# A spectral filter with a mixture of experts on one core: eight groups of batches become four

## The chip, the cores and the metric

One core of a Trainium2 chip runs the whole kernel. The metric is the device time of one execution in microseconds. Of three runs of the kernel before, the median is 1513.49 us (1512.85 to 1513.52).

## What is computed

Eight batches of 2496 positions with 256 channels are filtered along the positions: a real Fourier transform, a product with a complex filter per frequency and channel, and the transform back. Each of the 19,968 filtered rows is a token that goes to one of eight experts: the one with the largest cosine to its embedding. The expert is a 256 to 1024 to 256 network with a ReLU, and its output is scaled by the expert's softmax weight.

```python
X = np.fft.rfft(x, axis=1)                       # x: (8, 2496, 256)
y = np.fft.irfft(X * (filt_r + 1j * filt_i), n=2496, axis=1)
...
x = y.reshape(19968, 256)
logits = normalized(x) @ normalized(expert_emb).T / tau
expert_idx = np.argmax(logits, axis=1)
gate_w = softmax(logits)[np.arange(N), expert_idx]
for e in range(8):
    mask = expert_idx == e
    out[mask] = gate_w[mask, None] * (np.maximum(x[mask] @ w1[e], 0) @ w2[e])
```

## The kernel before

**The filter.** 2496 is 64 x 39, so the transform is done as two small DFTs each way. Stage one (`conv_s1`, L384) reads tiles of three times 39 positions, multiplies each with a block of DFT-39 factors, and stores the spectrum's parts to the DRAM buffer `SD`. The middle stage (`conv_s2`, L405) reads them back by frequency (`a`), does a DFT-64 product on TensorE, multiplies with the filter on VectorE (`yy` with the real, `xs` with the imaginary part, L432 and L434; `f` is the filter slice read by `load_f`, 256 KB), does the inverse DFT-64 product (`sa`), and stores to the DRAM buffer `ZD`. The last stage (`conv_sb`, L493) reads `ZD`, does the inverse DFT-39 product (`y`), normalizes and splits the rows into f16 high and low halves, transposes them (half by DMA, half on TensorE), and computes the logits. `route` (L613) turns every four tiles of logits into ranks, and GpSimd scatters each tile's rows with an indirect DMA (L697) into `XS`, a DRAM buffer with a region per expert.

A tile is always 512 columns wide. In a group of one batch it holds two blocks of rows or two frequencies of that batch; in a group of two batches (`GROUPS[g][0] == 2`) it holds one block or one frequency of both. So a step of the middle stage reads two filter slices in the first case (`k * 2 // nb`, L419), and one in the second. A product is either one f32 product, or, from a group number on (`G_S1`, `G_S2`, `G_SA`, `G_SB` for the four stages), split in three products of fp32r halves that ScalarE and VectorE make (`split`, L343).

**The experts.** `Slot` (L786) is a block of 128 or 256 tokens of one expert: rows are read transposed from `XS` (`xT`), then in four quarters of the hidden units `prep` copies weights (`wp`, VectorE), `up` multiplies (`ph`, L830), ScalarE and VectorE make the two halves of `h` (L836, L837), and `down` multiplies again (`po`, L850). ScalarE scales, GpSimd scatters the output rows (L858).

**What sets the order.** `GROUPS` says for every group how many batches it has and the size of the blocks that its tokens fill. A group that is filtered and routed adds to a queue as many full blocks as are sure to exist whatever the routing (`full_blocks`, L53, used at L86 to L94); what is left of the tokens goes to a last phase of 128-token blocks. While a queue runs, `spread` (L932) weaves steps of the next group's filter between the quarters of the blocks; `pace` divides the group's steps over the queue. The first group's filter runs alone (`head`, L890): its steps, numbered from 0, also carry the 16 weight loads (`WLOADS` gives step and number) and the 48 steps of weight preparation (`weight_halves`, L228: largest value of each matrix, scales, f16 high and low halves), at a rate given by the lines at L914. The first stage of group g + 1 is woven into the last stage of group g (`later`, L875).

With `GROUPS = ((1, 128),) + ((1, 256),) * 7` the queues are 12 blocks of 128 and 6, 10, 10, 9, 10, 10 and 10 of 256 tokens; then the last phase, in which 19 blocks of 128 run.

## Time and profile before

| | |
|---|---|
| median of 3 runs | 1513.49 us (1512.85 to 1513.52) |
| the profiled execution: its time | 1514.53 us |
| its span, first to last instruction | 1512.4 us |
| TensorE busy | 1282.9 us, 85% |
| VectorE, ScalarE, GpSimd busy | 66%, 52%, 36% |
| mean granted clock of TensorE | 0.903 of 2.4 GHz |
| bytes moved by DMA | 240.91 MB |

PE is TensorE, PEld its weight loads, DVE is VectorE, ACT ScalarE, POOL GpSimd, SP the engine that issues most DMAs. The granted clock is the share of 2.4 GHz that TensorE had on average; it has two levels, 1.2 and 2.4 GHz. A busy share over the whole span mixes three different stretches, so most of the rows below are of windows of time.

### The profile page before, as it was taken

The numbers are of one execution on the slowest core, as the hardware profiler recorded it, in microseconds if no ns is written. First come the engines' busy times: TensorE is split into PE (matmuls) and PEld (weight loads), VectorE is DVE, ScalarE is ACT, GpSimd is POOL, SyncE is SP. The second block draws the span as 40 slices with busy tenths as digits, with TensorE's granted clock in tenths as the row PEclk, the third lists the DMA queues.
The fourth block names the chain that finished last, engine by engine and source line by source line (L and its number), as shares of the span: only waits on it lengthen the run. The fifth ranks groups of instructions, "written<-read, shape, count | busy, mean of one in ns | idle before, by whom it ended". The sixth has DMA issues, their size and how long they took to land.

```text
span 1512.4 us, 36347 instructions
## 1 busy us (share of the span) xinstructions
PE 1282.9 (85%) x10678; PEld 983.3 (65%) x10678; DVE 992.1 (66%) x3238; ACT 781.9 (52%) x1781; POOL 551.1 (36%) x613
## 2 busy tenths in 40 slices
PE   4543649877998898898989997999899988999998
PEld 1111326654665576676877775787778766888998
DVE  3765658656574776696767784878578755444565
ACT  2653626643572576376735693568456732233333
POOL 0121544154425433552444435443454145121222
PEclk7765759987998898999999998999999998999999
DMA  9882858856894797577655895669465633222121
GB/s 302 304 279 64 193 145 246 187 136 190 221 192 134 212 218 148 149 215 185 161 137 154 214 206 141 166 200 207 114 182 177 132 88 89 52 52 46 43 48 41
DMA packets 278909, 240.91 MB, mean 159 GB/s; under 512 B 173977, under 2 KB 220385, under 8 KB 276933
## 3 DMA queue, kind: packets, MB, share of 16 engines
q1 hardware_dynamic: 248156, 161.38, 44.3%
q0 software_dynamic: 26400, 60.07, 13.6%
q10 hardware_dynamic: 4169, 17.12, 3.1%
q8 instruction: 102, 1.67, 0.5%
q14 instruction: 82, 0.67, 0.2%
HBM read 121.61 MB, written 84.84 MB: 137 GB/s over the span
## 4 chain that ended last, share of the span: by engine, by line
PE 55%; issue 13%; DMA 11%; DVE 10%; another core or an unknown queue 4%; ACT 4%; POOL 2%; SPq 0%; DVEq 0%; POOLq 0%; ACTq 0%
PE ph L830 20%; PE po L850 20%; PE s L382 4%; DMA out_dram<-o,meta 3%; PE y L382 2%; PE y L377 2%; PE s L377 2%; DMA f<-ZD 2%; DMA yT<-rows 2%; PE sa L382 2%; DVE wmx L235 1%; DMA f<-in_filt 1%; PE tp L584 1%; DMA SD<-s 1%
## 5 line engine op out<-in xcount | busy, mean ns | idle before, releaser
L830 PE MATMUL ph<-xT,wp 128*128 128x256 f16 (+1 forms) x4608 | 526.2, 262 | 28.7 <-issue 15.4
L850 PE MATMUL po<-W,h 128*128 x3864 | 518.4, 279 | 35.0 <-issue 25.1
L830 PEld LDWEIGHTS <-wp 128*128 128x128 f16 x4608 | 397.4, 100 | 125.6 <-issue 64.1
L850 PEld LDWEIGHTS <-h 128*128 128x128 f16 x3864 | 371.1, 100 | 118.9 <-issue 65.5
L836 ACT ACTIVATE h<-ph 128x512 f16<-128x512 f32 (+1 forms) x384 | 204.4, 533 | 311.6 <-PE ph L830 165.3
L818 DVE COPY wp<-W 128x1024 f16 x384 | 187.5, 489 | 222.0 <-PE ph L830 129.4
L858 POOL DMA_INDIRECT out_dram<-o,meta x161 | 171.5, 1065 | 390.0 <-ACT o L857 331.8
L837 DVE SCALAR_TENSOR_TENSOR h<-ph,h 128x512 f16<-128x512 f32 (+1 forms) x384 | 230.3, 600 | 50.7 <-ACT h L836 47.8
L697 POOL DMA_INDIRECT XS<-rows,ixi x176 | 177.9, 1011 | 173.9 <-issue 99.9
L468 POOL TENSOR_TENSOR yy<-yy,xs 128x512 f32<-128x512 f32 x70 | 94.5, 1351 | 113.1 <-DVE xs L434 85.7
L337 POOL DMA_DIRECT2D in<-in_x x84 | 66.3, 790 | 146.9 <-DVE xp L351 61.4
L857 ACT ACTIVATE o<-po,meta 128x256 f32<-128x256 f32 x161 | 69.8, 479 | 51.5 <-PE po L850 26.8
L536 DVE SCALAR_TENSOR_TENSOR rows<-y,rr,rows 128x256 f16<-128x256 f32 x176 | 76.9, 477 | 16.2 <-ACT rows L533 11.2
L533 ACT ACTIVATE rows<-y,rr 128x256 f16<-128x256 f32 x176 | 75.3, 492 | 21.1 <-DVE rr L570 19.2
L460 ACT COPY xs<-s 64x512 f32<-64x512 f32 x80 | 46.6, 582 | 76.4 <-PE s L377 63.7
L432 DVE TENSOR_TENSOR yy<-s,f 128x256 f32<-128x256 f32 x160 | 60.8, 416 | 37.5 <-ACT xs L461 30.2
L377 PE MATMUL s<-a,c_sb 128*128 128x512 f32 x80 | 51.5, 737 | 37.8 <-DVE yy L432 13.0
L565 ACT ACTIVATE rows<-y 128x256 f16<-128x256 f32 x176 | 67.5, 402 | 26.8 <-PE y L377 21.0
L377 PE MATMUL y<-f,csb_sb 120*128 120x512 f32 (+2 forms) x72 | 45.2, 718 | 37.3 <-issue 22.4
L434 DVE SCALAR_TENSOR_TENSOR xs<-xs,sgn_sb,f 128x256 f32<-128x256 f32 x160 | 76.1, 511 | 0.0
L400 ACT COPY s<-s 128x512 f32<-128x512 f32 x88 | 52.6, 599 | 30.1 <-DMA SD<-s 10.7
L382 PE MATMUL s<-xp,c1h 117*128 117x512 f32 (+1 forms) x144 | 62.2, 439 | 5.5 <-issue 3.3
(190 smaller groups left out, 1600.8 us busy)
## 6 DMA issues: line engine op xcount, KB each, us to landing
f<-in_filt SPq DMA_DIRECT2D x160, 256.0 KB
a<-SD SPq DMA_DIRECT2D x80, 256.0 KB
ZD<-z SPq DMA_DIRECT2D x80, 256.0 KB
SD<-s SPq DMA_DIRECT2D x80, 240.0 KB
f<-ZD SPq DMA_DIRECT2D x80, 240.0 KB
in<-in_x POOLq DMA_DIRECT2D x70, 234.0 KB
W<-in_w ACTq DMA_DIRECT2D x14, 1024.0 KB
XS<-rows,ixi POOLq DMA_INDIRECT x176
```

Of the source, the lines that this page charges most:

```text
L377: nc.tensor.matmul(out_, c[:a.shape[0]], a, start=True, stop=True)
L382: nc.tensor.matmul(out_, w[:k], b, start=(n == 0), stop=(n == 2))
L434: nc.vector.scalar_tensor_tensor(out=o, in0=i, scalar=sgn_sb[:, k2:k2 + 1], in1=f, op0=ALU.mult, op1=ALU.mult)
L468: nc.gpsimd.tensor_tensor(out=yy, in0=yy, in1=xs, op=ALU.add)
L536: nc.vector.scalar_tensor_tensor(out=rows[:, i, D:2 * D], in0=y[:, i], scalar=rr[:, u:u + 1], in1=rows[:, i, 0:D], op0=ALU.mult, op1=ALU.s ...
L697: i = nc.gpsimd.indirect_dma_start(out=XS, out_offset=bass.IndirectOffsetOnAxis(ap=ix, axis=0), in_=src, in_offset=None)
L818: last["dve"] = nc.vector.tensor_copy(wp, src[:, :, fp * 256:fp * 256 + 256])
L830: last["pe"] = nc.tensor.matmul(ph[:, fi, :size], wp[:, k * 2 + wh, fi * P:(fi + 1) * P], xT[:, xh * 2 + k], start=(c == 0), stop=(c == 5))
L836: nc.scalar.activation(h[:, 0, :, :size], ph[:, :, :size], AF.Relu)
L837: nc.vector.scalar_tensor_tensor(out=h[:, 1, :, :size], in0=ph[:, :, :size], scalar=0.0, in1=h[:, 0, :, :size], op0=ALU.max, op1=ALU.subtract)
L850: nc.tensor.matmul(self.po[:, s], self.hs[fp][:, hh, fi, s * P:(s + 1) * P], self.Wp[:, off + wh * 1024:off + wh * 1024 + D], start=(fp == ...
L858: i = nc.gpsimd.indirect_dma_start(out=out, out_offset=bass.IndirectOffsetOnAxis(ap=self.meta[:, s, 0:1].bitcast(I32), axis=0), in_=o, in_ ...
```

## The change

The groups become four of two batches each; the first has blocks of 128 tokens. The stages switch to split products at other group numbers: the first stage from group 1 (batch 2 on, as before), the other three from group 2 (batch 4 on; before, the middle stage's first product from batch 4 and the other two from batch 3). The weight loads are divided over the first 48 steps of the head instead of 33, and the weight preparation runs at one piece a step from step 16. `SMAX` limits a queue to 30 blocks, so that the table of a queue fits its buffer: the first group would have 32.

```diff
-GROUPS = ((1, 128),) + ((1, 256),) * 7
+GROUPS = ((2, 128),) + ((2, 256),) * 3
...
-G_S1, G_SB, G_S2, G_SA = 2, 3, 4, 3
+G_S1, G_SB, G_S2, G_SA = 1, 2, 2, 2
 DLAG = 2
 MID = 8
-WLOADS = {3: 1, 6: 1, 10: 2, 32: 2} | {n: 1 for n in range(12, 32, 2)}
+WLOADS = {3: 1, 6: 1, 10: 2} | {n: 1 for n in range(13, 48, 3)}
 WLATE = 6
+SMAX = 30
...
         left += n * S
-        k = full_blocks(left, size)
+        k = min(full_blocks(left, size), SMAX)
         phases.append((g, size, k, False))
...
-            if n >= 14 and not 44 <= n < 60:
-                owed += 1.5 if n < 60 else 1
+            if n >= 16:
+                owed += 1
             while owed >= 1:
                 owed -= 1
                 next(prep, None)
```

The queues are then 30 blocks of 128 and 17, 19 and 20 of 256 tokens, and the last phase as before. Line numbers after the new line are higher by one.

Two places of the order that the prediction speaks of. The first is VectorE's list in the middle stage of the head, at the filter products of step 7 (`yy_7`, `xs_7`; `W<-W` makes a low half of weights, `wmx` a largest value, `wall` waits for GpSimd). Before:

```order
L432 TENSOR_TENSOR yy_7_554<-s_0_7_549,f_14_493 128x256
L434 SCALAR_TENSOR_TENSOR xs_7_551<-xs_7_551,sgn_sb,f_14_493 128x256
L246 RECIPROCAL winv<-wsc 128x2
L235 TENSOR_REDUCE wmx<-W 128x1 x2
L241 TENSOR_SCALAR wall<-wall 128x2
L432 TENSOR_TENSOR yy_7_554<-s_0_7_549,f_15_495 128x256
L434 SCALAR_TENSOR_TENSOR xs_7_551<-xs_7_551,sgn_sb,f_15_495 128x256
```

And now:

```order
L433 TENSOR_TENSOR yy_7_606<-s_0_7_601,f_7_553 128x512
L435 SCALAR_TENSOR_TENSOR xs_7_603<-xs_7_603,sgn_sb,f_7_553 128x512
L264 SCALAR_TENSOR_TENSOR W<-W,wsc 128x1024
L242 TENSOR_SCALAR wall<-wall 128x2
L236 TENSOR_REDUCE wmx<-W 128x1 x2
L264 SCALAR_TENSOR_TENSOR W<-W,wsc 128x1024
L243 TENSOR_SCALAR wsc<-wall 128x2
L433 TENSOR_TENSOR yy_8_628<-s_0_8_623,f_8_579 128x512
```

A step had four products of 256 columns with two filter slices; it has two of 512 with one slice, and the weight work between them is the same in kind, with one piece a step.

The second is GpSimd's list while a queue of blocks runs and the last stage of the next group is routed (`XS<-rows` scatters a tile's rows, x2 for its two halves; `out_dram<-o` a block's output; `yy` is the sum of the two filter products in the middle stage). Before, in the third queue:

```order
L697 DMA XS<-rows_0_4489,ixi_0_5085 161920x258 x2
L697 DMA XS<-rows_1_4537,ixi_0_5085 161920x258 x2
L697 DMA XS<-rows_2_4638,ixi_0_5085 161920x258 x2
L697 DMA XS<-rows_3_4680,ixi_0_5085 161920x258 x2
L858 DMA out_dram<-o_3_0_5837,meta_3_4955 19968x256
L858 DMA out_dram<-o_3_1_5842,meta_3_4955 19968x256
L697 DMA XS<-rows_4_4741,ixi_4_5411 161920x258 x2
L697 DMA XS<-rows_5_4816,ixi_4_5411 161920x258 x2
L697 DMA XS<-rows_6_4879,ixi_4_5411 161920x258 x2
L697 DMA XS<-rows_7_4996,ixi_4_5411 161920x258 x2
```

And now, in the first queue:

```order
L698 DMA XS<-rows_15_6358,ixi_12_7082 161920x258 x2
L859 DMA out_dram<-o_24_0_7574,meta_24_7155 19968x256
L469 TENSOR_TENSOR yy_0_8382<-yy_0_8382,xs_0_8379 128x512
L698 DMA XS<-rows_16_6544,ixi_16_7680 161920x258
L469 TENSOR_TENSOR yy_1_8426<-yy_1_8426,xs_1_8423 128x512
L698 DMA XS<-rows_16_6544,ixi_16_7680 161920x258
L469 TENSOR_TENSOR yy_2_8455<-yy_2_8455,xs_2_8452 128x512
L698 DMA XS<-rows_17_6690,ixi_16_7680 161920x258 x2
L859 DMA out_dram<-o_25_0_7802,meta_25_7365 19968x256
L698 DMA XS<-rows_18_6817,ixi_16_7680 161920x258
```

Eight row scatters in one run were the rule, three runs to a batch; now they stand in ones and twos between output scatters and the next group's sums. Over the queues with filter work, runs of six or more hold 113 of 154 row scatters before and 21 of 132 in the change.

## Rows read from the trace of the kernel before

**Rows 1.** The profile's page: busy time of each engine with its share of the span and its instructions; and TensorE's busy share in 40 equal slices of the span, in tenths.

```profile
PE 1282.9 (85%) x10678; PEld 983.3 (65%) x10678; DVE 992.1 (66%) x3238; ACT 781.9 (52%) x1781; POOL 551.1 (36%) x613
...
PE   4543649877998898898989997999899988999998
```

**Rows 2.** Windows, cut where the first hidden product of each queue's first block is made on VectorE: the head, the seven queues that run beside a filter, the last queue, the last phase. Columns: window and its length in us, then busy us and number of instructions of each engine, granted clock, busy share of the DMA engines, GB/s.

```profile
0.00:226.80 226.80, 109.20 (x322) 42.70 (x323) 135.05 (x441) 98.43 (x180) 59.15 (x75) 0.67 0.69 215
226.80:366.40 139.60, 119.07 (x1100) 85.86 (x1098) 93.01 (x360) 73.52 (x192) 57.32 (x66) 0.88 0.74 187
366.40:494.30 127.90, 112.32 (x825) 78.20 (x822) 73.98 (x290) 66.82 (x165) 53.99 (x63) 0.92 0.76 183
494.30:675.70 181.40, 163.47 (x1267) 125.04 (x1267) 135.86 (x431) 111.57 (x253) 78.14 (x83) 0.92 0.76 191
675.70:842.10 166.40, 153.34 (x1269) 122.66 (x1268) 118.15 (x381) 98.03 (x225) 69.41 (x75) 0.95 0.67 165
842.10:994.10 152.00, 137.17 (x1144) 109.49 (x1143) 114.93 (x372) 95.02 (x220) 66.14 (x73) 0.96 0.72 181
994.10:1146.80 152.70, 144.42 (x1239) 117.29 (x1237) 115.30 (x375) 95.97 (x222) 65.92 (x72) 0.98 0.69 177
1146.80:1298.20 151.40, 134.73 (x1171) 109.94 (x1171) 96.39 (x366) 71.40 (x172) 56.87 (x65) 0.94 0.43 106
1298.20:1403.00 104.80, 104.80 (x963) 93.93 (x961) 47.23 (x80) 32.27 (x60) 19.54 (x20) 1.00 0.25 51
1403.00:1512.40 109.40, 104.34 (x1399) 98.18 (x1396) 62.22 (x151) 38.88 (x97) 24.62 (x21) 0.99 0.18 43
```

**Rows 3.** Windows of the hidden product on VectorE alone (L837, four to a block): the last queue of 256-token blocks (40 products, ten blocks), and 18 of the last phase's 128-token blocks (71 products begin inside, the 72nd ends the window). Columns: window and length, VectorE's busy us and instructions, granted clock, DMA share, GB/s.

```profile
1298.20:1403.00 104.80, 27.66 (x40) 1.00 0.25 51
...
1403.00:1498.60 95.60, 30.39 (x71) 1.00 0.20 46
```

**Rows 4.** Pieces of the chain of waits, with start, us and what: one f32 product of the middle stage (two instructions), and a split one of the first stage (three); and the timeline of TensorE with start, us and instructions, from the transposes of a last-stage tile over its eight logits products to the next product.

```profile
381.74 0.86 PE s L377 x2
...
462.16 0.70 PE s L382 x3
...
165.40 0.39 PE L584 MATMUL tp<-ident,rows 128*128 128x128 f16 x4
...
165.83 1.10 PE L377 MATMUL s<-in,c_sb 117*128 117x512 f32 x2
```

**Rows 5.** Windows of the head, columns as in rows 2: the first stage, the gap until the middle stage's first product, the middle stage, the last stage while weights are still being prepared, the last stage after that.

```profile
0.00:29.00 29.00, 17.45 (x28) 5.89 (x28) 8.37 (x36) 7.96 (x15) 1.06 (x10) 0.81 0.89 285
29.00:41.00 12.00, 0.00 (x0) 0.02 (x1) 8.17 (x16) 0.34 (x1) 0.73 (x2) 0.50 0.91 332
41.00:121.00 80.00, 40.68 (x60) 13.08 (x60) 58.47 (x115) 45.20 (x56) 15.44 (x13) 0.69 0.77 269
121.00:160.00 39.00, 13.56 (x31) 5.84 (x32) 17.37 (x43) 18.92 (x38) 11.41 (x14) 0.54 0.30 82
160.00:182.00 22.00, 17.85 (x106) 8.60 (x106) 18.71 (x101) 15.92 (x48) 7.45 (x13) 0.81 1.01 218
```

**Rows 6.** Groups of VectorE's instructions by line: count, busy us and mean ns of one, and the idle time before them with what ended it. The two filter products, the split's low half, the weights' largest values and low halves; and from the list of who waited for whom (us in total, times, longest) VectorE's scales waiting for GpSimd's largest value over all partitions.

```profile
L434 DVE SCALAR_TENSOR_TENSOR xs<-xs,sgn_sb,f 128x256 f32<-128x256 f32 x160 | 76.1, 511 | 0.0
L432 DVE TENSOR_TENSOR yy<-s,f 128x256 f32<-128x256 f32 x160 | 60.8, 416 | 37.5 <-ACT xs L461 30.2 <-issue 3.1 <-DMA f<-in_filt 2.7
L351 DVE TENSOR_TENSOR xp<-in,xp 117x512 fp32r<-117x512 f32 (+1 forms) x72 | 46.9, 654 | 25.8 <-ACT xp L350 19.8 <-ACT o L857 2.7 <-PE ph L830 1.3
...
L235 DVE TENSOR_REDUCE wmx<-W 128x1 f32<-128x1024 f32 x28 | 32.8, 1211 | 12.9 <-DMA W<-in_w 12.8
L263 DVE SCALAR_TENSOR_TENSOR W<-W,wsc 128x1024 f16<-128x1024 f32 x21 | 26.6, 1280 | 0.1
...
DVE wall L241 <- POOL wall L238: 36.4, 6, 10.9
```

**Rows 7.** Timeline of the head (start, us, instruction, and in brackets the engine's idle time before it and what ended it): a late inverse product of the middle stage, the copy for the last store of that stage, and the last stage's first, fifth and eleventh tile.

```profile
114.92 2.04 PE L486 MATMUL sa<-yy,m_sb 128*128 128x512 f32 x2 [11.58 <-DVE yy L432]
...
118.70 0.58 ACT L489 COPY z<-sa 128x512 f32<-128x512 f32 x1 [6.14 <-PE sa L486]
...
125.14 2.08 PE L377 MATMUL y<-f,csb_sb 120*128 120x512 f32 x2 [6.47 <-DMA f<-ZD]
...
159.78 2.05 PE L377 MATMUL y<-f,csb_sb 120*128 120x512 f32 x2 [3.04 <-issue]
...
181.36 1.30 PE L377 MATMUL y<-f,csb_sb 120*128 120x256 f32 x4 [1.22 <-PE s L377]
```

**Rows 8.** Windows, columns as in rows 2. The first and the last of the fifteen stretches with six or more row scatters on GpSimd without a break (each to 1.5 us behind its last one; the last is that of the dummy rows), and the sum over the fifteen; the sum over two last stages whose scatters stand in short runs (747.7 to 802.9 and 1060.4 to 1114.5 us); and the whole of the seven queues.

```profile
328.80:337.80 9.00, 5.93 (x61) 4.60 (x60) 2.34 (x14) 2.04 (x6) 6.99 (x7) 0.88 0.39 114
...
1268.50:1279.90 11.40, 7.56 (x49) 4.87 (x47) 1.79 (x10) 0.00 (x0) 7.77 (x8) 0.80 0.42 127
sum 154.50, PE 111.12 PEld 82.52 DVE 63.27 ACT 34.02 POOL 110.19; mean PE 7.41 PEld 5.50 DVE 4.22 ACT 2.27 POOL 7.35
...
sum 109.30, PE 96.76 PEld 77.73 DVE 66.96 ACT 46.49 POOL 58.67; mean PE 48.38 PEld 38.87 DVE 33.48 ACT 23.25 POOL 29.33
...
226.80:1298.20 1071.40, 964.54 (x8003) 748.48 (x8001) 747.63 (x2567) 612.33 (x1444) 447.78 (x497) 0.93 0.68 170
```

**Rows 9.** Timeline of TensorE inside such a stretch (907.4 to 917.9 us).

```profile
914.68 0.38 PE L830 MATMUL ph<-xT,wp 128*128 128x256 f16 x2 [1.04 <-issue]
```

## The prediction

> **What bounds the kernel now.** I read the page first. TensorE is busy 85% of the span and no other engine more than 66% [rows 1]; its slices are at 3 to 6 tenths in the first six, near full after that. So there are three stretches, and each wants its own account. The windows cut at the first hidden product of each queue of blocks [rows 2] show them: a head of 226.8 us in which only the filter of the first batch runs and TensorE works 109.2; seven queues of blocks with a later batch's filter woven in, 1071.4 us in all; and a tail of 214.2 us (104.8 + 109.4) of blocks alone, TensorE full, VectorE at 45 to 57%. In the head nothing is full for long: DMA 0.89 to 0.91 at first, VectorE 58.5 of 80 us in the middle DFT, the DMA engines again (1.01) in the last DFT [rows 5]. In the woven stretch TensorE is the bound but leaves 107 us idle, and its granted clock is 0.88 to 0.98, that is part of the time at the lower of its two levels.
>
> The prices. A block of 256 tokens takes 10.48 us (ten in 104.8 us), one of 128 takes 5.31 (18 in 95.6 us) [rows 3]. A filter product in f32 takes 0.86 us of TensorE at the high level, the three of a split one 0.70; the transposes and logits of a tile 0.43 [rows 4]. By these a batch costs 17.2 us for the two middle products (10 each), 14.2 for the last DFT (11 tiles), 7.7 for its split first DFT; all split, 14.0, 12.4 and 7.7. Blocks and filter of the seven queues come to 102.8, 102.0, 140.5, 138.9, 128.4, 138.9 and 131.2 us: 882.7 of the 1071.4 that they took. The first two took 267.5 for 204.8, a ratio of 1.306, with 0.61 us of filter for each us of blocks; the last four 622.5 for 537.4, or 1.158, with 0.31.
>
> **The change, part by part.**
>
> *Number of blocks.* The rule of the phases gives 30 blocks of 128 (32, cut to 30), then 17, 19 and 20 of 256, and the same 1792 tokens for the last phase: 56 + 30 instead of 65 + 12. That is 18 x 5.31 - 9 x 10.48 = +1.3 us. The Trainium skill (Perfetto Trace Analysis, Optimizing Tensor Performance) says that larger matmuls are more efficient than smaller ones, which speaks against trading 256 columns for 128. Here two half blocks cost 10.62 for 10.48 [rows 3], so the sum has 1.3 us; if a half block cost as much as a whole one, it would have +94.
>
> *Tail.* 20 x 10.48 + 19 x 5.31 and the 8.5 us that the old tail has beyond its own blocks: 319 us, **+105**. It is cover that moves out of the woven stretch.
>
> *Head.* First DFT: 22 tiles instead of 11 and seven weight loads of 1.05 MB instead of four, 17.7 MB with the constants; at 285 GB/s of the first 29 us [rows 5] that is 62 us. The gap of 12 us until the first middle product stays: 74. Middle DFT: 20 steps. One step now reads one filter slice instead of two, so 0.77 MB, and nine weight loads lie in them: 24.8 MB at 269 GB/s, 4.6 us a step. VectorE: the weights' largest values and low halves are 59.4 us and about 10 for the quarter pieces; some 23 of it stands ahead of the first step in the new order of VectorE's instructions, 47 in the steps; a step's own products are 0.76 + 0.95 us [rows 6] (before four instructions of 256 columns, now two of 512; I take no gain), 34 in 20; four waits for GpSimd's largest-of-all-partitions at 6.1 each [rows 6], 24. Together 105, or 5.2 us a step. Before it was 7.8 a step (41 to 119 us), with 2.3 MB in each. I take 5.2, since both loads of a step fell; bounds 4.6 and 7.8. Ends at 178. The first tile of the last DFT comes 6.4 us behind the last middle store now (125.1 against 118.7) [rows 7], so 184. Its tiles come every 3.6 us once the weights are out of the way (159.8 to 181.4, six) and every 5.6 with them [rows 7]. They are out of the way now, but the first DFT of the next group is woven in at 0.85 tiles each instead of 0.73 and is split, some 0.7 us of VectorE a tile [rows 6]: 4.2, bounds 3.6 and 5.6. 21 x 4.2 = 88: 272. From the last tile to the first block's hidden product it is 45.4 us (routing, slot table, read): **318, +91**. Bounds 293 and 399, the upper one only if both old paces came back.
>
> *Woven stretch.* Queues of 30, 17 and 19 blocks, each with two batches. 159.3 + 2 x 31.4 + 15.4 = 237.5; 178.2 + 68.2 = 246.4; 199.1 + 52.8 = 251.9; together 735.8. Batch 1's filter and the first DFT of batches 2 and 3 have gone into the head; batch 3's third and last DFT lose the split, which is 3.4 us more of TensorE and some 15 less of VectorE, the latter worth nothing where TensorE sets the pace. Filter per us of blocks is 0.49, 0.38 and 0.27. On the line between the two ratios above that gives 1.244 and 1.190 for the first two; for the third I take 1.154, the ratio of the old seventh queue (151.4 for 131.2 at 0.25), which the line would undercut: 295.5 + 293.2 + 290.7 = 879.4.
>
> *Row scatters.* In the fifteen stretches where GpSimd issues six or more row scatters without a break, TensorE is idle 43.4 of 154.5 us; in the rest of the woven stretch 63.5 of 916.9. In two stretches of the same work where the scatters come broken up it is 12.5 of 109.3 [rows 8]. TensorE starts a product or two at a time there, with pauses for which the trace shows no releaser [rows 9]. The excess, less the dummy rows' stretch that stays, is some 30 us. In the order of GpSimd's instructions, runs of six or more hold 113 of 154 scatters before and 21 of 132 after, since a longer group spreads them between other work. So 30 x 92/113 = **-24**: 855. Bounds: 0, if the stop belongs to a scatter wherever it stands, and -30.
>
> *Filter reads.* 80 slices of 0.26 MB less. In the woven stretch the DMA engines are at 0.68 [rows 8], so I cost this at nothing; the cover is that slack. A load that is late next would be the read of a block's rows behind the group's last scatter, which on GpSimd's queue now stands behind the sums of the next group's first eight steps.
>
> *Sum* against the profiled span: +91 (head), -216 (1071.4 to 855), +105 (tail) = -20, so 1492.4. The profiled run took 2.1 us beyond its span, 1514.5, about 1.0 above the median of 1513.5. The forecast on the median's footing is **1493 us**, 1.3% faster.
>
> **The rivals.**
>
> *The mixture keeps its loss (slower).* The woven stretch as a whole takes 1.214 of its blocks and filter (1071.4 / 882.7). If that holds, with no gain from broken runs, it takes 893 us: 318 + 893 + 319 = 1530, 1531 as measured. The place is the four or five engines' handshakes in the last DFT. For it: the ratio was 1.291 in the third queue, at only 0.34 of filter, so density is not all. Against it: the last four are at 1.158 and their queues are the ones most like the new. It decides from a woven stretch of 873 us on (1510 as measured). The Trainium skill (Perfetto Trace Analysis, Identifying Performance Opportunities, Optimization Strategy) says that where the most-contended engine changes between regimes, interleaving them may help; this change takes some 196 us out of the interleaving, to both ends. By that rule this rival is the likelier; the traces so far bear out that the ends lengthen, not that the middle fails to shrink.
>
> *The middle DFT of the head stays at 7.6 us a step (slower).* Steps wait in a row (product, ScalarE copies, VectorE with weight work ahead of it in its queue, second product) and not side by side: +48, 1541. For it: TensorE sat up to 11.6 us for VectorE there [rows 7], and its granted clock was 0.69 [rows 5], so that a step's three f32 products at the lower level are near 5.1 us too. Against it: DMA and VectorE are loaded much less per step. It decides from 6.1 us a step on. [...]
>
> *The woven queues run as well as the best one now (faster).* The sixth took 152.7 for 138.9, 1.099. 735.8 x 1.099 = 809: 318 + 809 + 319 = 1446, 1447 as measured. For it: three changes of queue instead of seven, broken runs, fewer reads. Against it: only one of seven did so.
>
> That the groups are not what the words say is excluded by the order of the change: 30, 17, 19 and 20 blocks stand in it.
>
> **How the numbers follow.** A change under 0.2% (3 us) can hardly be told from none here. Forecast 0.46 (of it 0.43 faster by more, 0.03 within), best-queue rival 0.12 (faster), mixture rival 0.24 (0.20 slower, 0.04 within), head rival 0.18 (0.12 slower, 0.02 within, 0.04 faster where the step is only a little longer). Faster 0.59, same 0.09, slower 0.32. The forecast's own range is 1475 to 1510 (steps of 4.6 to 6.0 us, scatter term 0 to 30). For 8 in 10 I go to half-way into the fast rival and to the mixture rival: 1462 to 1530.
>
> **What would show it.** Right: first hidden product near 318 us; middle steps at 5.2 us and last-DFT tiles at 4.2 in the head; three queues of about 290, 285 and 280 us; no long idle of TensorE in the scatters; a tail of 319 us. Wrong: a head beyond 340, or a woven stretch above 873 us, which is where the gain is gone.

## The result and the profile after

The change took 1528.07 us (median of six runs, 1521.17 to 1530.71) where the kernel before took 1513.17 beside it: a ratio of 1.0093 with a 95% interval of 1.0065 to 1.0121. It is **slower by 0.9%**, or 15 us; 1.3% faster was forecast. The profiled execution took 1528.63 us with a span of 1526.8. In two of the five later sessions, one of them on a chip that showed both in turn, the kernel before took 1387 us and not 1514 (below called the sessions without stops, since their traces lack pauses of TensorE and VectorE without a known releaser that the others have between the blocks), so ratios are taken within a session only.

The page of the change, busy time of each engine and TensorE's busy share in 40 slices, which answers to [rows 1]:

```profile
PE 1300.8 (85%) x11066; PEld 991.5 (65%) x11066; DVE 991.0 (65%) x3009; ACT 772.9 (51%) x1774; POOL 533.4 (35%) x585
...
PE   5355656659989888899989899999998899999998
```

The low part is now nine slices long instead of six. Windows of the change, bounded as [rows 2] and [rows 5] say (columns as there): first DFT; middle DFT; last DFT; from its last tile to the first block; the three woven queues together; the last queue; the last phase.

```profile
0.00:58.50 58.50, 32.35 (x48) 10.66 (x48) 22.59 (x62) 18.24 (x29) 3.92 (x13) 0.80 0.91 308
67.90:191.00 123.10, 70.22 (x118) 24.53 (x119) 83.18 (x134) 71.45 (x98) 21.06 (x19) 0.81 0.57 187
198.70:309.60 110.90, 73.35 (x352) 37.01 (x352) 65.17 (x328) 52.79 (x166) 43.24 (x63) 0.64 0.72 176
309.60:352.20 42.60, 24.43 (x115) 11.89 (x112) 29.59 (x129) 13.61 (x31) 24.30 (x25) 0.58 0.55 157
...
352.20:1210.10 857.90, 787.39 (x7146) 623.35 (x7145) 633.35 (x2048) 510.81 (x1232) 377.17 (x405) 0.96 0.62 156
1210.10:1418.80 208.70, 208.70 (x1920) 187.12 (x1919) 93.95 (x160) 64.31 (x120) 39.07 (x40) 1.00 0.24 51
1418.80:1526.80 108.00, 102.52 (x1377) 96.52 (x1374) 61.11 (x150) 38.47 (x96) 24.65 (x21) 1.00 0.21 43
```

Head 352.2 us (318 forecast), woven stretch 857.9 (855), tail 316.7 (319).

The bounds of the windows in [rows 2], from the second queue on, stand one hidden product too early. The one at 366.4 us still has the 256 columns of a 128-token block; the first with the 512 of a 256-token block is at 376.0. Both lines of VectorE in the kernel before, and its woven stretch with the bound moved by one product:

```profile
366.36 0.41 DVE L837 SCALAR_TENSOR_TENSOR h<-ph,h 128x256 f16<-128x256 f32 x1
...
376.04 0.69 DVE L837 SCALAR_TENSOR_TENSOR h<-ph,h 128x512 f16<-128x512 f32 x1 [0.26 <-ACT h L836]
```

```profile
226.80:1300.80 1074.00, 967.14 (x8027) 750.81 (x8025) 748.75 (x2569) 612.92 (x1445) 447.78 (x497) 0.94 0.68 170
```

That leaves 211.6 us for the tail. Against this the change has +125.4, -216.1 and +105.1, where +91, -216 and +105 were forecast. **All of the miss is in the head.** It has two parts: 123.1 / 20 = 6.15 us for a middle step (5.2 forecast), and 110.9 / 21 = 5.28 for a tile of the last DFT (4.2 forecast). No engine is full in either window and the DMA engines are at 0.57 and 0.72, so something is waited for.

A step's own products on VectorE are a little cheaper than in [rows 6], two of 512 columns instead of four of 256 (1.43 us of busy time a step; [rows 6] gives 0.76 + 0.95 = 1.71 before):

```profile
L435 DVE SCALAR_TENSOR_TENSOR xs<-xs,sgn_sb,f 128x512 f32<-128x512 f32 x80 | 59.6, 744 | 0.0
L433 DVE TENSOR_TENSOR yy<-s,f 128x512 f32<-128x512 f32 x80 | 54.8, 686 | 35.3 <-ACT xs L462 28.6 <-issue 5.3 <-DMA ZD<-z 1.3
```

Who waited for whom in the middle DFT (67.9 to 191 us; total, times, longest):

```profile
DVE wall L242 <- POOL wall L239: 33.8, 6, 10.1
PE sa L487 <- DVE yy L433: 31.6, 6, 8.1
...
POOL wall L239 <- issue: 27.4, 3, 10.8
POOL W L261 <- issue: 24.0, 3, 8.7
...
DVE W L264 <- ACT W L263: 11.6, 4, 6.5
...
ACT W L260 <- POOL W L261: 4.1, 1, 4.1
DVE yy L433 <- ACT xs L462: 3.6, 1, 3.6
```

And two stops in the timelines of GpSimd, VectorE and TensorE (start, us, instruction, idle time before it and what ended it), the first of the six and a later one:

```profile
68.41 0.17 DVE L242 TENSOR_SCALAR wall<-wall 128x2 f32<-128x2 f32 x1 [10.09 <-POOL wall L239]
...
93.62 0.14 DVE L237 TENSOR_REDUCE wmax<-wmx 128x1 f32<-128x2 f32 x1
...
100.78 0.37 POOL L239 PARTITION_ALL_REDUCE wall<-wmax  x1 [8.17 <-issue]
101.19 0.17 DVE L242 TENSOR_SCALAR wall<-wall 128x2 f32<-128x2 f32 x1 [6.16 <-POOL wall L239]
...
105.97 0.69 DVE L433 TENSOR_TENSOR yy<-s,f 128x512 f32<-128x512 f32 x1
...
106.72 1.22 PE L487 MATMUL sa<-yy,m_sb 128*128 128x512 f32 x1 [7.66 <-DVE yy L433]
```

VectorE stands at a scale of the weights until GpSimd has the largest value over all partitions. The weight work and the filter product behind it in VectorE's queue are late, and TensorE waits 7.66 us for that. GpSimd was idle for 8.17 us, the last 7 of them after VectorE's part was done at 93.8, and waited for nothing that the profile shows. The stop that ends at 68.41 lies ahead of the first step but for 0.5 us, so 24.2 of the 33.8 us are in the middle DFT. There VectorE also waits for ScalarE: 11.6 us for high halves of weights, in the rows above, and 3.6 for copies of the spectrum. The longest of these waits, 6.5 us, stands behind a cast on ScalarE that waited 4.1 us for a late subtraction on GpSimd (both waits in the rows above).

In the order of GpSimd's instructions a row without an operand stands wherever the kind of work changes (L239 is the reduction, L261 the subtraction for a low half of weights):

```
16 L261 TENSOR_TENSOR W<-W 128x1024
17 L239 ISA
18 L239 ISA wall<-wmax 128x2 x2
19 L261 ISA
20 L261 TENSOR_TENSOR W<-W 128x1024 x2
```

Of the eight reductions three follow another one, or nothing; they begin 0.1 us after VectorE's part. The five that follow a subtraction begin 5.9 to 11.3 us after it. A subtraction and the two reductions behind it:

```profile
55.11 2.13 POOL L261 TENSOR_TENSOR W<-W 128x1024 f16<-128x1024 f32 x1 [10.97 <-ACT W L260]
68.00 0.37 POOL L239 PARTITION_ALL_REDUCE wall<-wmax  x1 [10.77 <-issue]
76.36 0.35 POOL L239 PARTITION_ALL_REDUCE wall<-wmax  x1 [7.99 <-DVE wmax L237]
```

In the last DFT (198.7 to 309.6 us) TensorE waits for the cast with which ScalarE begins the split of the next group's first stage:

```profile
PE s L383 <- ACT xp L351: 24.1, 16, 3.0
```

### The profile page after: what moved, and what is told of

Same layout as the page of the kernel before. It is cut to its first block, busy times and chain, and to the rows that moved or that the text cites. A ratio compares the mean times of both kernels' runs of the same rounds, so it can differ in the third digit from the quotient of the medians.

```text
span 1526.8 us, 37113 instructions
## 1 busy us (share of the span) xinstructions
PE 1300.8 (85%) x11066; PEld 991.5 (65%) x11066; DVE 991.0 (65%) x3009; ACT 772.9 (51%) x1774; POOL 533.4 (35%) x585
## 3 DMA queue, kind: packets, MB, share of 16 engines
q1 hardware_dynamic: 219014, 142.96, 38.3%
## 4 chain that ended last, share of the span: by engine, by line
PE 49%; issue 10%; DMA 7%; DVE 6%; ACT 2%; POOL 2%; another core or an unknown queue 0%; DVEq 0%; SPq 0%; POOLq 0%; ACTq 0%
PE ph L831 20%; PE po L851 20%; DMA out_dram<-o,meta 3%; PE s L383 2%; PE y L383 2%; DVE xs L435 1%; DVE wp L819 1%; DMA XS<-rows,ixi 1%; POOL out_dram L859 1%; DMA f<-ZD 1%; DVE h L838 1%; PE sa L487 1%; POOL yy L469 1%; PE s L378 1%; PE tp L585 1%
## 5 line engine op out<-in xcount | busy, mean ns | idle before, releaser
L851 PE MATMUL po<-W,h 128*128 x3864 | 509.5, 277 | 25.7 <-issue 16.1
L831 PE MATMUL ph<-xT,wp 128*128 128x256 f16 (+1 forms) x5040 | 505.7, 250 | 26.4 <-issue 13.5
L837 ACT ACTIVATE h<-ph 128x512 f16<-128x512 f32 (+1 forms) x420 | 209.0, 500 | 339.9 <-PE ph L831 195.7
L819 DVE COPY wp<-W 128x1024 f16 x420 | 214.5, 511 | 199.7 <-PE ph L831 140.8
L698 POOL DMA_INDIRECT XS<-rows,ixi x176 | 186.8, 1061 | 170.6 <-issue 88.1
L469 POOL TENSOR_TENSOR yy<-yy,xs 128x512 f32<-128x512 f32 x60 | 82.7, 1381 | 115.0 <-DVE xs L435 97.8
L338 POOL DMA_DIRECT2D in<-in_x x66 | 54.1, 819 | 130.0 <-DVE xp L352 56.1
L487 PE MATMUL sa<-yy,m_sb 128*128 128x512 f32 x80 | 50.4, 716 | 44.0 <-DVE yy L433 31.6
L378 PE MATMUL y<-f,csb_sb 120*128 120x512 f32 (+1 forms) x88 | 65.1, 832 | 18.2 <-DMA f<-ZD 11.6
L433 DVE TENSOR_TENSOR yy<-s,f 128x512 f32<-128x512 f32 x80 | 54.8, 686 | 35.3 <-ACT xs L462 28.6
L490 ACT COPY z<-sa 128x512 f32<-128x512 f32 x80 | 46.6, 582 | 48.6 <-PE sa L487 36.0
```

Source lines behind the costliest of these rows:

```text
L378: nc.tensor.matmul(out_, c[:a.shape[0]], a, start=True, stop=True)
L469: nc.gpsimd.tensor_tensor(out=yy, in0=yy, in1=xs, op=ALU.add)
L698: i = nc.gpsimd.indirect_dma_start(out=XS, out_offset=bass.IndirectOffsetOnAxis(ap=ix, axis=0), in_=src, in_offset=None)
L819: last["dve"] = nc.vector.tensor_copy(wp, src[:, :, fp * 256:fp * 256 + 256])
L831: last["pe"] = nc.tensor.matmul(ph[:, fi, :size], wp[:, k * 2 + wh, fi * P:(fi + 1) * P], xT[:, xh * 2 + k], start=(c == 0), stop=(c == 5))
L837: nc.scalar.activation(h[:, 0, :, :size], ph[:, :, :size], AF.Relu)
```

## The experiments

Head, woven stretch and tail are bounded as above. "Before" is the kernel before in the same session.

| run | median us | before | ratio, 95% interval | head | woven | tail |
|---|---|---|---|---|---|---|
| e1_plain_first | 1506.98 | 1514.74 | 0.9951 [0.9923, 0.9979] | 329.6 | 856.8 | 316.5 |
| e2_scales_later | 1515.62 | 1514.74 | 1.0012 [0.9985, 1.0039] | 340.4 | 847.2 | 316.6 |
| e3_both | 1494.56 | 1514.74 | 0.986 [0.9826, 0.9895] | 322.9 | 855.9 | 316.4 |
| e5_later_pairs | 1516.59 | 1514.74 | 0.9996 [0.9966, 1.0026] | 223.5 | 977.6 | 316.4 |
| a2_change_again | 1525.2 | 1513.84 | 1.0085 [1.0053, 1.0116] | 351.6 | 861.9 | 316.7 |
| e3_again | 1496.04 | 1513.84 | 0.9886 [0.9841, 0.9931] | 323.7 | 854.6 | 316.9 |
| **e8_again** | **1473.62** | 1513.84 | **0.9747 [0.9713, 0.9782]** | 300.4 | 857.6 | 316.7 |
| e7_again | 1488.47 | 1513.84 | 0.9846 [0.9811, 0.9881] | 202.6 | 1071.6 | 212.0 |
| e3_third | 1499.54 | 1514.23 | 0.9898 [0.986, 0.9936] | 323.7 | 858.8 | 317.0 |
| e6_runs_third | 1563.23 | 1514.23 | 1.033 [1.029, 1.037] | 323.2 | 919.3 | 316.7 |
| *sessions without stops* | | | | | | |
| e8_no_switch | 1399.79 | 1387.23 | 1.0095 [1.0062, 1.0128] | 281.1 | 800.6 | 316.3 |
| e4_later_single | 1453.83 | 1387.23 | 1.0483 [1.0449, 1.0517] | 294.8 | 940.4 | 212.1 |
| e6_runs | 1425.51 | 1387.23 | 1.0273 [1.0242, 1.0305] | 299.7 | 802.4 | 316.5 |
| e7_before_mended | 1360.46 | 1387.23 | 0.9805 [0.9772, 0.9839] | 192.7 | 957.8 | 211.6 |
| e6_runs_again | 1423.21 | 1386.21 | 1.0259 [1.0202, 1.0316] | 297.5 | 804.8 | 316.4 |
| e4_single_again | 1454.26 | 1386.21 | 1.048 [1.0423, 1.0536] | 295.2 | 940.6 | 212.4 |
| e11_filter_twice | 1437.89 | 1386.21 | 1.0355 [1.0291, 1.0419] | 307.9 | 811.1 | 316.7 |
| e13_switch_alone | 1400.57 | 1386.21 | 1.0096 [1.0041, 1.0151] | 283.3 | 796.7 | 316.3 |

**e1_plain_first: the split in the last DFT.**

```diff
-G_S1, G_SB, G_S2, G_SA = 1, 2, 2, 2
+G_S1, G_SB, G_S2, G_SA = 2, 2, 2, 2
```

> The change, with the first stage of the second group (woven into the last stage of the head) as one f32 product instead of a split one. Theory A: of the head's 352 us some 20 are the split's cast and low half on ScalarE and VectorE, for which TensorE waited 16 times in the last DFT: the tiles there come at about 4.3 us instead of 5.28, the first hidden product near 332, the time about 1508 us. Rival B (the head is held by the DMA engines, the low clock and the row scatters): tiles stay at 5.1 to 5.4 us and the time within 3 us of 1528; with the longer f32 products at the low clock it may be 5 us worse.

Its last DFT (columns as before):

```profile
198.90:287.80 88.90, 57.85 (x336) 27.61 (x336) 51.00 (x305) 43.35 (x147) 41.35 (x63) 0.83 0.95 218
```

88.9 / 21 = 4.23 us a tile: the forecast's 4.2, which only holds without the split. The head is 22.6 us shorter. TensorE's granted clock in the window went from 0.64 to 0.83, nearer to its level of 2.4 GHz, and the DMA engines from 0.72 to 0.95. The rival is out.

**e2_scales_later: VectorE's stops.**

```diff
+        for j in range(2):
+            largest(0, j)
+            yield
         for e in range(E):
-            for j in range(2):
-                largest(e, j)
-                yield
+            if e + 1 < E:
+                for j in range(2):
+                    largest(e + 1, j)
+                    yield
             scales(e)
```

> The change, with the pieces of weight preparation in another order: the largest values of expert e+1 stand ahead of the scales of expert e, so that VectorE comes to a scale two pieces after GpSimd was asked for the largest value over all partitions. Nothing is left out. Theory A: the middle DFT of the head loses the six stops of VectorE for GpSimd (33.8 us) and ends some 25 to 30 us earlier, about 4.8 us a step instead of 6.15; head near 325, time about 1500 us. Rival B (a step is held by its chain of product, copy, filter product and store, or by the DMA engines): the stops vanish and other waits take their place, steps stay above 5.8 us, time above 1520 us.

Half of it came: the first tile of the last DFT is at 185.2 us instead of 198.7, the time 10 to 12 us lower. The stops were not gone (middle DFT, 69 to 178 us):

```profile
DVE wall L242 <- POOL wall L239: 22.4, 4, 10.2
```

Being asked earlier helps little where GpSimd itself is late: it still goes back and forth between reductions and subtractions. The expected 1500 us was 15 too low.

**e3_both** (both edits) and its repeats e3_again, e3_third.

> Both edits together: weight pieces in the new order, and the second group's first stage unsplit. Theory A: the two gains lie in different stages of the head and add up: head near 305 us, time about 1480, which is 2% below the kernel before. Rival B: above 1515 us. If only one of the two causes holds, about 1500.

> The change with both edits, on the same chip as the change itself and the kernel before. Where before takes 1514: 1492 to 1500, ratio 0.984 to 0.99. Where it takes 1387: 1415 to 1428 (as the run with scatters in long runs), ratio 1.02 to 1.03.

> The change with both edits, as the base of e6_runs_third. Where the kernel before takes 1514: 1494 to 1497 as measured twice. Where it takes 1387: 1418 to 1428, since row scatters in runs of eight would cost nothing there.

1494.56, 1496.04 and 1499.54 us: the gains in the head add up but for 5 us. That this is close to the forecast's 1493 is chance, since it is another program. The expectation of 1480 was too low by what e2 fell short.

**e8_no_switch, e8_again, e13_switch_alone: one kind of work on GpSimd.** On top of e3_both:

```diff
-                if j == 0:
-                    nc.scalar.activation(raw, raw, AF.Copy, scale=sc)
-                    nc.scalar.copy(hi, raw)
-                    nc.gpsimd.tensor_tensor(out=lo, in0=raw, in1=hi, op=ALU.subtract)
-                else:
-                    nc.scalar.activation(hi, raw, AF.Copy, scale=sc)
-                    v.scalar_tensor_tensor(out=lo, in0=raw, ...)
+                nc.scalar.activation(hi, raw, AF.Copy, scale=sc)
+                v.scalar_tensor_tensor(out=lo, in0=raw, ...)
```

> As e3_both, and the low half of a matrix's first quarter is made by VectorE's fused multiply and subtract, like the other three quarters, and not by ScalarE and GpSimd; so GpSimd does nothing but the largest values over all partitions until the last DFT. Theory S (the VectorE stops that are left, 21.5 us in the middle DFT of e3_both, come from GpSimd changing between two kinds of program: 7 to 10 us without a releaser stand ahead of each, and the order of its instructions has a row without a name there): the stops go, the middle DFT ends some 10 to 15 us earlier although VectorE gets 8 x 1.28 us more, head about 310, time about 1482. Rival (the reduction over partitions itself takes that long, or the step's own chain holds the pace): head 320 to 326, time 1492 to 1500.

> As e3_again with the low halves on VectorE alone. Theory S: 12 to 20 us below e3_again on either kind of chip, all of it in the head.

> As e8_no_switch without the new order of the pieces: the change with the second group's first stage unsplit and all low halves on VectorE; scales are asked for right behind the largest values, as in the change. If GpSimd's change of program alone made the stops long: 1473 to 1480, as e8_again (0.973 to 0.978 of the kernel before where that takes 1514). If the look-ahead is needed, because the reduction itself takes some microseconds: 1484 to 1500, with stops of 3 to 5 us for each expert.

The edit also takes one of two passes over these weights off ScalarE. Middle DFT and last DFT of e3_again, and then those of e8_again:

```profile
68.80:183.80 115.00, 73.84 (x120) 25.87 (x120) 81.08 (x123) 71.64 (x99) 25.38 (x19) 0.78 0.60 200
190.40:279.70 89.30, 58.44 (x335) 28.08 (x336) 51.69 (x307) 43.18 (x148) 41.63 (x63) 0.83 0.96 217
```

```profile
71.10:160.90 89.80, 65.56 (x119) 22.65 (x120) 80.50 (x129) 63.30 (x90) 7.12 (x9) 0.90 0.76 256
...
167.70:259.50 91.80, 64.24 (x336) 30.62 (x336) 51.88 (x309) 43.99 (x148) 42.82 (x64) 0.76 0.92 214
```

A largest value in e8_again on VectorE, GpSimd's reduction of it, and the scale that needs it:

```profile
91.02 0.15 DVE L237 TENSOR_REDUCE wmax<-wmx 128x1 f32<-128x2 f32 x1
...
91.26 1.32 POOL L239 PARTITION_ALL_REDUCE wall<-wmax  x1 [18.56 <-DVE wmax L237]
...
96.19 0.16 DVE L242 TENSOR_SCALAR wall<-wall 128x2 f32<-128x2 f32 x1
```

The reduction is done at 92.6, 1.4 us after VectorE's part, and no idle time stands before the scale; in the change 7 us lay between the two (93.6 to 100.8). All eight reductions begin 0.1 us after VectorE's part, in e13_switch_alone too. The middle DFT takes 89.8 us, or 4.5 a step, about the lower bound that the prediction worked out from bytes (4.6), though VectorE makes nine low halves more; it is busy for 80.5 of them. The time falls by 22.4 us, the head by 23.3. e13_switch_alone has no look-ahead and took 1400.57 us, or 1.0096 of its kernel before, to e8_no_switch's 1399.79 and 1.0095 in the other session of the same kind (its expected times are for a session with stops, in which it did not run). GpSimd's own stops are in those sessions too: in e6_runs a reduction behind a subtraction begins up to 9.4 us after VectorE's part. So it is the change of kind on GpSimd that cost, not the reduction. The Trainium skill (GPSIMD Engine Reference, Terminology) has loadable kernel libraries that a DMA brings in while the program runs; the trace agrees in so far as up to 10.8 us without a releaser stand before a reduction and up to 8.7 before a subtraction, and go when nothing changes. That the stops are such loads no run here shows. e8_again is **2.5% faster than the kernel before**, the best of its session.

**a2_change_again** (no edit).

> The change itself, beside the kernel before on one chip once more, since the kernel before took 1387 us on the chip of the last four runs and 1514 on the others, with waits of VectorE on 'remote' and of TensorE on 'issue' that the faster chip's traces don't have. If those stops are there again (before near 1514): ratio 1.006 to 1.013, as first measured. If they are not (before near 1387): the stops that the change took out of the woven stretch cost nothing there, so the ratio is worse: 1425 to 1450 us, 1.027 to 1.045.

1525.2 us, ratio 1.0085: the first result stands.

**e7_before_mended, e7_again: the mends alone, in the kernel before** (the diffs of e2 and e8 on it).

> The kernel before (eight single groups) with the two edits to its weight preparation alone: the largest values one expert ahead of the scales, low halves on VectorE and not on GpSimd. If the stops of VectorE for GpSimd (36.4 us in six) hold the head of the kernel before as they hold that of the change: head 205 to 215 and time 1495 to 1503. Rival (its head waits for filter slices and the last DFT's DMA, the stops lie beside that): head 223 to 228, time 1510 to 1516.

> The kernel before with its weight preparation mended in the same way. Where before takes 1387: 1360 as measured, below e8_again by 39. Where it takes 1514: 1483 to 1495, so that mended pairs (e8_again, near 1478) and mended singles are within 10 us of each other, or the pairs are ahead.

Its head falls from 226.8 to 202.6 us and its time by 25 us, more than was expected. So in the end single groups with the mend take 1488.5 and pairs 1473.6 in one session, a gain of 15 us for the change; in a session without stops they take 1360.5 and 1399.8, a loss of 39. What turns the order round lies in the woven stretch: 1071.6 us with stops are 957.8 without for singles, and 857.6 are 800.6 for pairs.

```profile
202.60:1274.20 1071.60, 966.58 (x8024) 748.32 (x8022) 749.96 (x2572) 613.16 (x1445) 446.87 (x497) 0.94 0.69 170
```

```profile
192.70:1150.50 957.80, 917.07 (x8027) 733.86 (x8026) 755.75 (x2572) 614.22 (x1445) 445.47 (x497) 0.98 0.76 190
```

(The first is e7_again, the second e7_before_mended: the same program and the same 8,000 products.)

**e6_runs, e6_runs_again, e6_runs_third: row scatters in runs of eight.** On e3_both:

```diff
-            if out_rows:
-                out_rows.pop(0)()
+            while out_rows:
+                out_rows.pop(0)()
+                if not g:
+                    break
```

> As e3_both, but the row scatters of groups 1 to 3 are given to GpSimd all at once when they are due, so that of the 132 woven ones most stand in runs of eight again (runs of six or more hold 126 and not 21). Theory T (the term of the prediction: TensorE stops in long runs): the woven stretch grows by some 20 to 26 us, time about 1517. Rival (a stop belongs to a scatter wherever it stands, or to the end of a group): 1490 to 1499, woven stretch 850 to 857 as in e3_both.

> As e6_runs: the change with both edits, and row scatters of groups 1 to 3 given out in runs of eight. Where the kernel before takes 1514: theory T (TensorE stops in long runs) has the woven stretch at 873 to 880 instead of 853 and the time near 1517, 1.002 of before; the rival 1490 to 1500, 0.985 to 0.991. Where it takes 1387: 1.027 again.

> The same with row scatters of groups 1 to 3 in runs of eight. Where the kernel before takes 1514: theory T has 1512 to 1522 (woven stretch 873 to 880), the rival 1490 to 1500. Where it takes 1387: 1424, and within 6 us of e3_third by both, as TensorE's pauses without a releaser are not in those traces.

Without stops its woven stretch is that of e8_no_switch (802 to 805 us, 801 there); e3_both itself was not run in those sessions. With them it is 64 us slower than e3_third beside it, 919.3 against 858.8 woven. Two of thirteen stretches with six or more scatters, to 1.5 us behind the last, and the thirteen together, of e6_runs_third and then of e6_runs_again:

```profile
498.90:510.60 11.70, 5.72 (x57) 3.85 (x54) 1.41 (x7) 0.00 (x0) 8.19 (x9) 0.71 0.58 154
561.20:572.60 11.40, 4.70 (x52) 3.15 (x49) 2.06 (x12) 0.72 (x2) 7.81 (x8) 0.83 0.36 97
...
sum 150.70, PE 92.48 PEld 63.97 DVE 55.09 ACT 40.89 POOL 112.39; mean PE 7.11 PEld 4.92 DVE 4.24 ACT 3.15 POOL 8.65
```

```profile
724.10:736.20 12.10, 12.10 (x118) 9.99 (x115) 9.10 (x26) 10.36 (x28) 9.73 (x12) 1.00 1.04 199
748.90:760.90 12.00, 12.00 (x118) 10.25 (x116) 8.87 (x24) 9.06 (x24) 9.32 (x9) 1.00 1.08 185
...
sum 154.90, PE 143.94 PEld 122.06 DVE 114.52 ACT 93.01 POOL 122.58; mean PE 11.07 PEld 9.39 DVE 8.81 ACT 7.15 POOL 9.43
```

Over the thirteen, TensorE has 802 products in 150.7 us with the stops and 1532 in 154.9 without. VectorE's and ScalarE's busy time halves too, while GpSimd's scatters take the same time (1010 and 1030 ns each, over the whole kernel). Which of the three engines is held first, and by what, is not shown. The waits show where the releaser is unknown (woven stretch; e6_runs_third, then e3_third):

```profile
PE po L857 <- issue: 25.7, 35, 1.9
PE ph L837 <- issue: 24.3, 38, 1.9
...
DVE wp L825 <- remote: 71.5, 12, 10.3
```

```profile
PE po L855 <- issue: 20.7, 28, 1.8
...
PE ph L835 <- issue: 9.9, 17, 1.3
...
DVE wp L823 <- remote: 36.7, 10, 6.9
```

None of these kinds is among the seven longest of either engine in e6_runs_again. Theory T holds, and the price, 60.5 us, is 2.5 times what the prediction gave, though runs of six or more hold 102 of the 132 scatters here, not the 126 of the expectation. Its range for the time, 1512 to 1522, was far too low. Long runs are not all: with short ones (857.6 to 800.6) another 57 us go with the session.

**e11_filter_twice: filter reads.** On e3_both, for the later groups:

```diff
                 nc.sync.dma_start(ft, filt[k2])
+                if g:
+                    nc.sync.dma_start(ft, filt[k2])
```

> As e3_both, but in groups 1 to 3 each filter slice is read twice, the second time into the same place (60 more reads of 0.26 MB, 15.7 MB). The term of the prediction (80 reads fewer are worth nothing): within 4 us of e3_both, 0.985 to 0.991 of the kernel before. Rival (they are work of the DMA engines that is waited for): 8 to 15 us more.

The woven stretch is 811.1 us beside 804.8 (e6_runs_again) and 796.7 (e13_switch_alone) of its session, at a DMA share of 0.74: 6 to 14 us for 60 reads. Its head is some 10 longer than that of e6_runs_again (the last tile to the first block, 45.6 against 38.3 us, where the second group's first slices are read), its tail the same; in all it is 14.7 us slower. e3_both itself was not run in that session, so the price is not exact; but the rival's 8 to 15 fits better than the term's nothing.

**e5_later_pairs and e4_later_single: which groups are pairs.** The first is on the kernel before, the second on e3_both:

```diff
-GROUPS = ((1, 128),) + ((1, 256),) * 7
+GROUPS = ((1, 128), (1, 256)) + ((2, 256),) * 3
```

```diff
-GROUPS = ((2, 128),) + ((2, 256),) * 3
+GROUPS = ((2, 128),) + ((1, 256),) * 6
```

The group numbers from which products are split are set along with them (not shown): the last three stages split from batch 4 on in both.

> The kernel before, with its first two groups left as single batches and only the last six batches in pairs: groups of 1, 1, 2, 2, 2 batches; the head is that of before. Theory A (the loss is all in the head; pairs do no harm where they are woven): head 227 us as before, the queues a little shorter than those of before through broken scatter runs, 1485 to 1508 us. Rival C (the gain in the woven stretch came only from work that moved to the ends): same as before, 1508 to 1520 us. Rival D (pairs cost in the mixture): above 1520 us.

> As e3_both, but only the first two batches are a pair; the other six are groups of one, with blocks of 256 and queues of 7, 10, 9, 10, 10 and 10 of them. Theory P (the gain of the woven stretch is only work that stands at the ends and a larger cover, pairs as such give nothing): 1487 to 1502, with a head a few us shorter (half as many first-stage tiles woven in). Rival Q (pairs shorten the woven stretch, by broken scatter runs and fewer handovers, 24 us in the prediction): 1508 to 1525.

> As e4_later_single: only the first group is a pair. Where the kernel before takes 1514: if pairs give in the woven stretch what they gave on the faster chip (28 us), 1520 to 1530; if the stops there weigh on single groups more, 1530 to 1560; if pairs give nothing there, 1487 to 1502. Where it takes 1387: 1.048 again.

e5 came out at the same time as before, in rival C's range, and tells little: its second queue has 6 blocks for the filter of a pair, so TensorE runs out of blocks there:

```profile
380.80:599.00 218.20, 168.04 (x1096) 110.87 (x1093) 138.64 (x521) 128.34 (x315) 103.01 (x119) 0.82 0.78 198
```

218.2 us for 62.9 of blocks (137.1 in the kernel before, beside a single batch). Whether the later pairs gain anything beside that, it does not show. e4 is 28 us slower than e6_runs beside it (woven +138, tail -104.4, head -4.9), in a session without stops, so there, behind a first pair, pairs in the later groups are worth something; what, and how much with the stops, stays open, as both runs fell in sessions of that kind.

## Why the prediction was wrong

The sum failed in one stretch, the head: +91 forecast, +125.4 measured. By its steps:

- *First DFT and gap:* 74 forecast, 67.9 measured (first DFT 58.5, gap 9.4), -6.
- *Middle DFT, 105 us or 5.2 a step:* **waits for ScalarE were left out, and GpSimd's stops taken as a fixed price.** It took 123.1: VectorE's products 28.6 (34 forecast), weight work 54.6 (47; the stop ahead of the first step pushed 9 us of it in front of the first filter product), waits for GpSimd 24.2 (24, so rightly sized), and waits for ScalarE 15.2, for which the sum had nothing. 6.15 a step, first tile at 198.7 and not 184 (+15, the -6 included). The prediction added up VectorE's work as if the engines that feed it were ready. GpSimd's instructions had no account of their own, though the move put all of the weight preparation into the first and middle DFT; without its changes of kind both sorts of wait nearly go (4.1 us in all in e8_again, 39.4 here) and a step takes 4.5, the lower bound.
- *Last DFT, 4.2 us a tile:* **mis-sized.** The split was priced as 0.7 us of VectorE; what came on the path was ScalarE's cast, for which TensorE waits 16 times, and TensorE's lower clock in the waits. Together 5.28, or +23 for 21 tiles; unsplit it is 4.23.
- *Last tile to first block:* 45.4 forecast, 42.6 measured.
- *Woven stretch, 855:* right as a sum (857.9), **wrong in its parts.** The run with long scatter runs shows 60.5 us where the prediction had 24 for a similar number of scatters (81 taken out of long runs, 92 there). So by that run blocks and filter with long runs would have been near 919 and not 879. Of the 39 us between them some 16 come from the bounds of [rows 2]: with each moved by one product the first two queues took 286.3 us for 204.8 of blocks and filter (1.398, not 1.306) and the last four 621.5 for 537.4 (1.156), and the prediction's own line then gives 308.0 + 298.2 + 288.8 = 895. The rest is ratios that were too low without a reason found. The scatter term was mis-sized because it counted TensorE's idle time alone, 43.4 us of [rows 8]; the time in which TensorE is shown busy with fewer products is lost too. [rows 8] had it: 61 and 49 products in its two stretches are 6.8 and 4.3 a us, against 7.5 over the seven queues. The two errors cancel, so the right sum was luck.
- *Filter reads at nothing:* not borne out; 60 more reads took 6 to 14 us of the woven stretch where no stops are. *Tail:* 316.7 for 319, and +105.1 for +105, right.

Of the rivals, the middle DFT of the head came nearest: it was to decide from 6.1 us a step on, and the step was 6.15, though at a clock of 0.81 and not 0.69, and with 19 of its 48 us. The mixture rival needed a woven stretch above 873 and did not get it; the third queue's 1.291, on which it leaned, is 1.183 by the right bounds (166.2 for 140.5). In a session without stops mended singles, with more work interleaved, beat mended pairs by 39 us (1360.5 to 1399.8). The Trainium skill (Perfetto Trace Analysis, Identifying Performance Opportunities, Optimization Strategy) says that interleaving stretches with different limits may help; these two runs agree, though they differ in more than that. What the session costs in the woven stretch, 114 us for singles (1071.6 to 957.8) and 57 for pairs (857.6 to 800.6), turns the order round. The best-queue rival needed a woven stretch of 809 us and did not get it.

## What to carry to other kernels

When work is moved into a stretch, account for every engine that it uses, and above all for an in-order queue that changes between kinds of work: a wait of 6 to 10 us there, as GpSimd showed here, holds whatever is queued behind the engine that asks. A long run of scatters that GpSimd issues itself can hold the other engines at half their rate, as it did in the session of e6_runs_third and not in that of e6_runs_again, so spread it, and price such a stretch by instructions per microsecond and not by idle time. Check that a window begins where its words say, by the shape of the instruction at its bound. A sum that comes out right may still hold two wrong terms; undo each part before trusting one.

## What the runs showed of the hardware

- GpSimd stands still for up to 10.8 us, without a releaser in the trace, when it changes between the reduction over partitions and an elementwise subtraction; leaving nine subtractions to VectorE took 22 us off the time.
- One and the same program took 1423 and 1563 us on one chip in two sessions (e6_runs_again, e6_runs_third), with equal times where blocks run alone (208.7 us for the last queue) and the difference mainly in the stretches with row scatters: 114.5 us in the woven stretch, 20 in the last DFT of the head. The 40 output scatters of the last queue cost nothing more. What differs between the sessions no run here shows.
- In long runs of row scatters TensorE makes 802 products against 1532, and VectorE and ScalarE are busy for half the time (55 against 115 us, 41 against 93), while GpSimd's own scatters take 1.0 us each in both.
